# An mLSTM cell and a squared-ReLU FFN on one core: squares on ScalarE, wider rounding, and half-depth matmuls in quarters of the array

## The chip, the cores and the metric

The kernel runs on one core of one Trainium2 chip. The metric is the device time of one execution in microseconds (us), as the median of several executions. Times inside an execution come from one profiled run; they count from the start of its span.

## What is computed

The reference is an mLSTM cell over 768 time steps for 4 batches of 8 heads of 40 elements, and a feed-forward network (FFN) with a squared rectifier on its output, seen as 3072 tokens of 320 elements.

```python
for t in range(S):                       # q, k, v, o_gate: (4, 8, 768, 40)
    m_new = np.maximum(f_gate[:, :, t] + m, i_gate[:, :, t])
    f_stab = np.exp(f_gate[:, :, t] + m - m_new)
    i_stab = np.exp(i_gate[:, :, t] - m_new)
    m = m_new
    C = f_stab[..., None, None] * C + i_stab[..., None, None] * einsum('bhd,bhe->bhde', vt, kt)
    n = f_stab[:, :, None] * n + i_stab[:, :, None] * kt
    h_tilde = einsum('bhde,bhe->bhd', C, qt)
    denom = np.maximum(np.abs(einsum('bhd,bhd->bh', n, qt)[..., None]), 1.0)
    y[:, :, t] = sigmoid(o_gate[:, :, t]) * h_tilde / denom
...
x = y.transpose(0, 2, 1, 3).reshape(3072, 320)
h = np.maximum(x @ w_in, 0.0)            # w_in: (320, 2048)
out = h * h @ w_out                      # w_out: (2048, 320)
```

The two weights arrive as 64-bit words and are rounded to 32 bits inside the kernel.

## The kernel before

The time steps are cut into 24 chunks of 128 tokens, numbered `s`; six chunks make one batch, and `c` is the chunk's place in its batch. Inside a chunk the recurrence is written as attention. `scores(s)` multiplies keys and queries of eight heads, two heads at a time, because one head fills only 40 of the 128 rows of TensorE's array. `weigh` turns gate sums into weights on ScalarE (`mask` on GpSimd goes before it), `weighted` multiplies scores and weights on VectorE, `attend_turned` multiplies the result with the values and with the state `C`, `normalise_turned` divides by the denominator and applies the output gate.

From chunk 7 on, keys and queries come already paired through DRAM: `load_squares(s)` fetches 32x32 blocks with four DMAs, and `turn_kq(s)` transposes them in place on VectorE (L318). There are two such buffers, used by even and by odd chunks. `load_squares(s + 2)` is issued in stage `s` on SyncE's queue behind `store_rows(s)`, which waits for `normalise_turned(s)`.

The FFN works on groups `g` of two chunks. Its first product of groups 0 to 2 is written plainly: `ffn1_main` and `ffn1_rest` fill two PSUM banks, `relu_half` writes the rectified values into SBUF tiles `r_sb` on ScalarE (L671), and `square_half` squares them on VectorE into the tile of squares (L678). From group 3 on both products use Winograd's form of Strassen's scheme: seven products of halves instead of eight, with sums of blocks prepared on VectorE and GpSimd. `ffn1_open` and `ffn1_close` make the first product in two quarters `q`; each takes four PSUM banks X, Y, V and Z. The last 64 of the 320 rows of `w_in` go through 64-row matmuls in `ffn1_close` (L845), two at a time in the lower and upper half of the array's rows. `ffn2_fast` makes the second product in four steps with two banks in steps 0 and 1 and two more in steps 2 and 3.

`Rounding` brings the weights in as 26 pieces: ten of `w_in`, 512 columns wide, and sixteen of `w_out`, 320 columns wide. A piece costs a DMA on SyncE's queue (`fetch`), two ScalarE operations (L196, L198), three on VectorE (L207, L211, L212) and one on GpSimd (L216). The tuples `NEXT` and `LAST` say how many pieces must be done after each part of the early loop and of the main loop.

The order of the work is written out by hand: each engine executes its instructions in the order in which the program issues them. The main loop takes the chunks from `s = 6` on; a stage `s` has four quarters, `at` = 0 to 3. The FFN part of a stage alternates: from `s = 8`, even stages run `ffn2_fast` of one group, one step in each quarter, and odd stages from `s = 9` run `ffn1_open`, `ffn1_close`, `ffn1_open`, `ffn1_close` of another (`fast`). Around it stand the attention's parts: at 0 `scores(s)` and `weighted(s)`; at 1 `attend_turned(s)`, then, among others, `turn_kq(s + 1)` and `turn_squares(s - 1)` (L615), and the loads; at 2 `scale_q(s + 1)` (L486), `weigh(s + 1)`, `normalise_turned(s)` (L568 to L577), `store_rows(s)`, `load_squares(s + 2)`, `load_rows(s)`, `load_A(s + 2)`; at 3 the sums of blocks of `x` on GpSimd. Sums of blocks of the squares (`sums`, L734) are spread over the quarters on VectorE.

In the main loop PSUM's eight banks are three for attention (`ps_at`) and five for the FFN (`ps_h`, tile `h_ps`).

Of the kernel before, what the change touches and what calls it, by code (L numbers as in the profile page):

```python
# [29 lines left out]
def kernel(  # L30
# [127 lines left out]
            ))  # L158
    IN_DONE = (3, 5, 8, 10)
    assert len(pieces) == IN_DONE[-1]  # L160
    pieces += [(w_out[:, fb, :], [(slice(0, P), wout_w[fb * P : (fb + 1) * P])]) for fb in range(NF)]
    NRAW = 4

    class Rounding:
# [11 lines left out]
        def fetch(self):  # L176
            n = len(self.raws)
            if n == len(pieces):
                return
            dst, srcs = pieces[n]  # L180
            raw = conv.tile([P, 512, 2], I32, name="raw", bufs=NRAW)
            self.raws.append(raw)
            for rows, src in srcs:
                to = raw[rows, : dst.shape[1]]
                if len(src.shape) == 4:
                    to = to.rearrange("p (a f) w -> p a f w", a=src.shape[1])
                nc.sync.dma_start(to, src)

        def words(self):
            n = len(self.a)  # L190
            if n == len(pieces):
                return
            w = pieces[n][0].shape[1]
            raw = self.raws[n][:, :w]
            mag = conv.tile([P, 512], F32, name="mag", bufs=3)
            nc.scalar.activation(mag[:, :w], raw[:, :, 1].bitcast(F32), AF.Abs)  # L196
            low = conv.tile([P, 512], F32, name="low", bufs=3)
            nc.scalar.activation(low[:, :w], raw[:, :, 0].bitcast(U32), AF.Copy, bias=2.0, scale=2.0 ** -51)  # L198
            self.a.append((mag, low))

# [80 lines left out]

    SQ = 32
    KQ_SQ, X_SQ = 7, 6

    def pair_up(s):
        b, c = divmod(s, NB)
# [112 lines left out]
            )  # L399

    def bank(o=False):
        t = ps_o.tile([P, W], F32, name="tp", tag="o_ps") if o else ps_at.tile([P, W], F32, name="tp", tag="at")
        return t[:].rearrange("p (j t) -> p j t", j=PR)

    def transposes(s, o=(False, False)):
# [10 lines left out]
    def scores(s, o=(False, False)):  # L416
        d = st[s]

        sc = [bank(o[i]) for i in range(2)]
        for j in range(PR):  # L420
            for i in range(2):
                rows = slice(DP * i, DP * i + D)
                nc.tensor.matmul(  # L423
                    sc[i][:, j, :], lhsT=d["kT"][rows, j, :], rhs=d["qT"][rows, j, :], start=True, stop=True,
                )
        d["sc"] = sc

    def weighted(s):
        d = st[s]
# [235 lines left out]
    def relu_half():  # L665
        if "half" in st:
            hs, g4 = st.pop("half")
            rs = []
            for h in hs:
                rs.append(ffn.tile([P, 2, WG], F32, name="r_sb", bufs=4))  # L670
                nc.scalar.activation(rs[-1][:], h[:], AF.Relu)  # L671
            st.setdefault("relu", []).append((rs, g4))

    def square_half():
        if st.get("relu"):
            rs, g4 = st["relu"].pop(0)
            for i, r in enumerate(rs):
                nc.vector.tensor_tensor(g4[:, :, i, :], r[:], r[:], op=ALU.mult)  # L678

    def ffn2(g, j, part):  # L680
        if part == 0:
# [129 lines left out]
    def blocks(to, lhsT, rhs, q, start):  # L811
        for n in range(4):
            nc.tensor.matmul(  # L813
                to[:, n, :], lhsT=lhsT[:, 4 * q + n, :], rhs=rhs, start=(start and n == 0), stop=True,
                skip_group_check=True,
            )
# [13 lines left out]
        nc.vector.tensor_tensor(U4[:], V[:], U2[:], op=ALU.add)  # L830
        blocks(Z, F22, xs[:, 4, :], q, True)

    def ffn1_close(g, q):
        xT, xs = st["xT", g], st["xs"]
        (X, Y, V, Z), (U2, U4) = st["f1"], st["U"]
        g4 = st["g2", g][:, 8 * q : 8 * q + 8, :].rearrange("p (n two) t -> p n two t", two=2)
        t0, t1 = slice(0, P), slice(P, 2 * P)
        blocks(X, F12, xT[:, 0, 1, :], q, False)
        blocks(Y, F21, xs[:, 2, :], q, True)
        blocks(V, WS[3], xT[:, 1, 1, :], q, True)  # L840
        lo, hi = slice(0, KR), slice(KR, 2 * KR)
        for pair in (((X, lo, xT[lo, 0, 2, :]), (Y, hi, xT[hi, 1, 2, :])), ((V, lo, xT[lo, 1, 2, :]), (Z, hi, xs[hi, 1, :]))):
            for n in range(4):
                for to, rows, rhs in pair:
                    nc.tensor.matmul(  # L845
                        to[:, n, :], lhsT=w_in2[rows, 4 * q + n, :], rhs=rhs, start=False, stop=True, skip_group_check=True,
                    )
        tt = nc.vector.tensor_tensor
        nc.scalar.activation(g4[:, :, 0, t0], X[:], AF.Relu)
        tt(U2[:], U2[:], Y[:], op=ALU.add)  # L850
        tt(g4[:, :, 1, t1], U4[:], Y[:], op=ALU.add)
        tt(g4[:, :, 0, t1], U4[:], V[:], op=ALU.add)
        tt(g4[:, :, 1, t0], U2[:], Z[:], op=ALU.subtract)
        st["open"] = g4
# [97 lines left out]
    rounding.step()  # L952


    NEXT = (5, 8, 10, 11, 13, 15, 17, 19)
    for u in range(8):
        s = 2 + u // 2
        relu_half()
# [63 lines left out]
    for g in range(1, NG):  # L1022
        parts += [(2, g, i) for i in range(4)]
        if g + 2 < NG:
            parts += [(1, g + 2, i) for i in range(4)]
    LAST = (21, 23, 25, 25, 26)
    assert LAST[-1] == len(pieces)
    for n, (which, g, i) in enumerate(parts):
        s, at = 6 + n // 4, n % 4
        if n == 5:  # L1030
            brought.close()
            late = ctx.enter_context(tc.tile_pool(name="late", bufs=1, side="right"))
        if at == 0:
            do(score, s)
        if at == 1:
            do(attend_turned, s)
            do(decays, s + 1)
            do(mask, s + 1)
            if n > 4:
                do(turn_kq, s + 1)  # L1040
            do(decay_C, s + 1)
            if s > X_SQ:
                do(turn_squares, s - 1)
            do(store_num, s)
            do(load, s + 4)
            if 8 <= s < 20:
                load_o(s + 4)
            do(load_num, s)
            do(pair_up, s + 3)
# [15 lines left out]
                sums_of_win(2 * (n - 10) + more)  # L1065
        if at == 3 and s >= 8 and s % 2 == 0 and s // 2 - 1 < NG:
            sums_of_x(s // 2 - 1)
        fast = which == 1 and g > 2
        if at == 2 and not fast:
            if n > 4:  # L1070
                do(scale_q, s + 1)
        if at == 3:
            if s % 4 == 3:
                for r in range(s + 1, min(s + 5, NT)):
                    sigmoid(r)
        if fast:
            (ffn1_close if i % 2 else ffn1_open)(g, i // 2)
            if at == 2:
                do(scale_q, s + 1)
        elif which == 1:  # L1080
            ffn1_main(g, i)
            if i % 2 == 0:
                held = st["half"]
            else:

                both = held, st["half"]
                for more, half in enumerate(both):
                    ffn1_rest(g, i - 1 + more, half[0])
                for half in both:
                    st["half"] = half  # L1090
                    relu_half()
                    square_half()
        elif g == 0:
            ffn2(g, *divmod(i, 2))
        else:
            ffn2_fast(g, i)
# [46 lines left out]
```

## Time and profile before

| | |
|---|---|
| median of 8 runs | 517.49 us (515.95 to 519.15) |
| the profiled execution | 516.24 us |
| its span, first to last instruction | 514.5 us |
| VectorE busy | 368.2 us (72%) |
| ScalarE busy | 237.9 us (46%) |
| GpSimd busy | 113.2 us (22%) |
| L678, squares on VectorE | 24 operations, 12.9 + 5.7 us |
| L671, rectifier on ScalarE | 24 operations, 12.7 us |
| L423, scores | 384 records, 27.0 us |
| L845, 64-row matmuls of the FFN | 576 records, 36.9 + 19.0 us |

A matmul of 32-bit operands appears as two records, each with a weight load of its own (engine PEld). "Busy" is the time in which at least one instruction of the engine or group runs, so for matmuls that overlap it is less than the number times the mean. The ends of matmuls are modelled; their starts are not.

### The profile page before, as it was taken

Reading aid. Unit: us, or ns where it says so; the run is one execution under the profiler, and the core shown is the slowest. Engines: PE = TensorE matmul, PEld = TensorE weight load, DVE = VectorE, ACT = ScalarE, POOL = GpSimd, SP = SyncE. Lnnn points to the kernel's source line nnn. Section 1 sums busy time; section 2 is a strip of 40 time slices with the busy share of each in tenths; the row PEclk is TensorE's granted clock in tenths of the full one; section 3 lists DMA queues with packets and bytes.
Section 4 is the critical chain, followed back from the end, with each engine's and each line's share of the span. In section 5 each row is a group of like instructions: output and inputs, shape, how many; then the busy total and the mean of one; then the engine's idle time right before and its main releaser. Section 6 shows DMA issues by size and latency. Waiting matters only on the chain.

```text
span 514.5 us, 11946 instructions
## 1 busy us (share of the span) xinstructions
PE 504.4 (98%) x4648; PEld 462.4 (90%) x4649; DVE 368.2 (72%) x678; ACT 237.9 (46%) x496; POOL 113.2 (22%) x146
## 2 busy tenths in 40 slices
PE   8989999999999999999999999999999999999997
PEld 4877878886698999999999999999999999999997
DVE  8589988969979777677768777668669667544441
ACT  3766667552531642571641681550771642432400
POOL 3346633233213103112112111112112112020000
PEclk9997999999999999999999999999999999999999
DMA  9999599786585776785785685785755353100000
GB/s 187 230 213 195 161 161 198 184 190 127 131 160 104 166 150 119 174 157 105 168 154 111 169 155 115 174 164 95 176 118 102 108 117 82 49 9 27 1 27 27
DMA packets 238361, 67.64 MB, mean 131 GB/s; under 512 B 185729, under 2 KB 232833, under 8 KB 238305
## 3 DMA queue, kind: packets, MB, share of 16 engines
q1 hardware_dynamic: 238208, 66.68, 61.8%
q8 instruction: 37, 0.61, 0.5%
q10 hardware_dynamic: 96, 0.20, 0.1%
q14 instruction: 20, 0.16, 0.1%
HBM read 54.56 MB, written 17.86 MB: 141 GB/s over the span
## 4 chain that ended last, share of the span: by engine, by line
PE 82%; DVE 9%; issue 2%; ACT 2%; DMA 2%; SPq 1%; POOL 0%; DVEq 0%; ACTq 0%; POOLq 0%
PE h_ps L739 32%; PE h_ps L813 21%; PE h_ps L845 7%; PE h_ps L645 4%; PE tp L423 4%; PE numT L522 3%; PE h_ps L685 3%; PE numT L513 2%; DVE mag L211 2%; PE hp L461 1%; DMA A_bc<-a_rows 1%; PE h_ps L656 1%; DVE g_c L678 1%; DVE mag L207 1%; DVE mag L212 1%
## 5 line engine op out<-in xcount | busy, mean ns | idle before, releaser
L361 POOL TENSOR_SCALAR_AFFINE_SELECT A_bc<-A_bc 128x1024 f32<-128x1024 f32 x22 | 24.3, 1106 | 213.4 <-ACT kq L371 185.6
L371 ACT ACTIVATE kq<-A_bc 64x512 f32<-64x512 f32 x30 | 18.8, 628 | 74.9 <-DMA A_bc<-a_rows 74.7
L739 PE MATMUL h_ps<-T,S 128*128 128x160 f32 x352 | 51.4, 299 | 0.0
L739 PE MATMUL h_ps<-w_out,g 128*128 128x160 f32 x336 | 49.2, 303 | 0.0
L739 PEld LDWEIGHTS h_ps<-T,S 128*128 128x128 f32 x352 | 49.0, 190 | 0.0
L385 ACT ACTIVATE A_bc<-A_bc,b_T 128x128 f32<-128x128 f32 x144 | 44.0, 389 | 7.6 <-POOL A_bc L361 7.0
L739 PEld LDWEIGHTS h_ps<-w_out,g 128*128 128x128 f32 x336 | 46.1, 190 | 1.1
L645 PE MATMUL h_ps<-xT,w_in 128*128 128x256 f32 x192 | 45.9, 395 | 0.6 <-ACT xT L624 0.6
L645 PEld LDWEIGHTS h_ps<-xT,w_in 128*128 128x128 f32 x192 | 37.0, 198 | 6.6 <-ACT xT L624 0.9
L813 PE MATMUL h_ps<-xT,w_in 128*128 128x128 f32 x288 | 40.7, 284 | 0.3 <-ACT r_sb L826 0.3
L813 PE MATMUL h_ps<-xs,w_in 128*128 128x128 f32 x288 | 38.0, 275 | 0.0
L813 PEld LDWEIGHTS h_ps<-xT,w_in 128*128 128x128 f32 x288 | 34.9, 191 | 3.4 <-ACT r_sb L826 0.5
L755 DVE TENSOR_TENSOR y_sb<-y_sb,h_ps 128x160 f32<-128x160 f32 x44 | 14.0, 318 | 33.2 <-PE h_ps L739 33.1
L826 ACT COPY r_sb<-h_ps 128x512 f32<-128x512 f32 x18 | 10.5, 584 | 58.0 <-PE h_ps L813 58.0
L845 PE MATMUL h_ps<-xT,w_in 64*128 64x128 f32 x432 | 36.9, 280 | 0.0
L845 PEld LDWEIGHTS h_ps<-xT,w_in 64*128 64x128 f32 x432 | 33.4, 187 | 2.2
L813 PE MATMUL h_ps<-xs,WS 128*128 128x128 f32 x288 | 35.1, 275 | 0.0
L813 PEld LDWEIGHTS h_ps<-xs,w_in 128*128 128x128 f32 x288 | 35.1, 192 | 0.0
L813 PEld LDWEIGHTS h_ps<-xs,WS 128*128 128x128 f32 x288 | 33.6, 192 | 0.0
L739 PE MATMUL h_ps<-w_out,g_c 128*128 128x160 f32 x192 | 28.0, 302 | 0.0
L850 DVE TENSOR_TENSOR r_sb<-r_sb,h_ps 128x512 f32<-128x512 f32 x18 | 12.3, 686 | 21.7 <-PE h_ps L845 21.7
L423 PE MATMUL tp<-kqT 40*128 40x128 f32 x384 | 27.0, 280 | 0.0
(167 smaller groups left out, 1070.0 us busy)
## 6 DMA issues: line engine op xcount, KB each, us to landing
A_bc<-a_rows SPq DMA_DIRECT2D x22, 512.0 KB, 4.8
raw<-in_moe_w_out_dram SPq DMA_DIRECT2D x16, 320.0 KB, 3.5
num_rows<-tn SPq DMA_DIRECT2D x18, 256.0 KB, 4.3
kq<-num_rows SPq DMA_DIRECT2D x72, 64.0 KB, 2.2
kqT<-kq_rows SPq DMA_DIRECT2D x34, 128.0 KB, 3.4
raw<-in_moe_w_in_dram SPq DMA_DIRECT2D x8, 512.0 KB, 5.6
kq<-in_k_dram SPq DMA_DIRECT2D x24, 160.0 KB, 5.0
va<-in_v_dram SPq DMA_DIRECT2D x24, 160.0 KB, 5.1
```

What stands on the lines that cost most here:

```text
L361: nc.gpsimd.affine_select(A[:], A[:], compare_op=ALU.is_ge, fill=-1e30, base=0, pattern=[[0, H], [1, P]], channel_multiplier=-1,)
L371: nc.scalar.activation(e[rows], st[s]["A"][0][rows, PR * i : PR * (i + 1), :], AF.Exp)
L385: nc.scalar.activation(d["W"][:, i * n + h, :], A[i][:, h, :], AF.Exp, bias=b_T[:, b, c, i * n + h : i * n + h + 1],)
L423: nc.tensor.matmul(sc[i][:, j, :], lhsT=d["kT"][rows, j, :], rhs=d["qT"][rows, j, :], start=True, stop=True,)
L522: nc.tensor.matmul(numT[i][halves[g], e, :], lhsT=va_w[s % NKQ][:, h * D1 : h * D1 + DP], rhs=d["P"][h % 2][:, h // 2, :] if s < KQ_SQ els ...
L645: nc.tensor.matmul(hs[i][:, n, :], lhsT=w_in[:, a, fb * P : (fb + 1) * P], rhs=xT[:, :, a, :], start=(n == 0 and a == 0), stop=False,)
L685: nc.tensor.matmul(o_ps, lhsT=st["g2", g][:, fb, j * P : (j + 1) * P], rhs=w_out[:, fb, :], start=(fb == 0), stop=(fb == NF - 1),)
L739: nc.tensor.matmul(to, lhsT=lhsT[:, p], rhs=rhs[:, p, :], start=(start and p == 0), stop=(p == NPAIR - 1), skip_group_check=True,)
L755: add = lambda to, a, b: nc.vector.tensor_tensor(to, a, b, op=ALU.add)
L813: nc.tensor.matmul(to[:, n, :], lhsT=lhsT[:, 4 * q + n, :], rhs=rhs, start=(start and n == 0), stop=True, skip_group_check=True,)
L845: nc.tensor.matmul(to[:, n, :], lhsT=w_in2[rows, 4 * q + n, :], rhs=rhs, start=False, stop=True, skip_group_check=True,)
L850: tt(U2[:], U2[:], Y[:], op=ALU.add)
```

## The change

In five places:

1. `relu_half` writes the rectified values straight into the tile of squares, and `square_half` squares that tile in place with one ScalarE operation of 1024 columns. The VectorE multiplications and the use of `r_sb` here go.
2. `w_out`'s pieces are two blocks wide (640 columns), so there are 18 pieces in all; the rounding tiles grow to 640 columns, and `NEXT` and `LAST` are renumbered.
3. From chunk 7 on `scores` makes each matmul in two, of 64 keys each, so that four matmuls (two heads, two halves of the keys) address the four quarters of the array.
4. For even `s` from 8 on, the scores of the odd chunk `s + 1` move into stage `s`: `turn_kq(s + 1)` goes from quarter 1 to quarter 0, `scores(s + 1)` stands at the head of quarter 1, into two banks of `ps_h`, and `weighted(s + 1)` in quarter 3. The odd stage begins with the FFN.
5. The 64-row matmuls move into a function `ffn1_rows`, each in two halves of 64 columns, in the order of the four quarters. In the first half of an odd stage they go to the head of quarter 1, ahead of `attend_turned`, and they, not F21 and WS[3], then clear the banks Y and V.

```diff
-    pieces += [(w_out[:, fb, :], [(slice(0, P), wout_w[fb * P : (fb + 1) * P])]) for fb in range(NF)]
+    pieces += [
+        (
+            w_out[:, fb : fb + 2, :].rearrange("p a d -> p (a d)"),
+            [(slice(0, P), wout_w[fb * P : (fb + 2) * P].rearrange("(a p) c w -> p a c w", p=P))],
+        ) for fb in range(0, NF, 2)
+    ]
+    WIDE = 2 * DM
...
+    HALVES = slice(0, DP), slice(DP, 2 * DP)
...
     def bank(o=False):
-        t = ps_o.tile([P, W], F32, name="tp", tag="o_ps") if o else ps_at.tile([P, W], F32, name="tp", tag="at")
+        if o == "h":
+            t = ps_h.tile([P, W], F32, name="h_ps")
+        else:
+            t = ps_o.tile([P, W], F32, name="tp", tag="o_ps") if o else ps_at.tile([P, W], F32, name="tp", tag="at")
...
+        if s >= KQ_SQ:
+            for j in range(PR):
+                for keys in HALVES:
+                    for i in range(2):
+                        rows = slice(DP * i, DP * i + D)
+                        nc.tensor.matmul(
+                            sc[i][keys, j, :], lhsT=d["kT"][rows, j, keys], rhs=d["qT"][rows, j, :], start=(j == 0),
+                            stop=True, skip_group_check=True,
+                        )
+            return
...
-            rs = []
-            for h in hs:
-                rs.append(ffn.tile([P, 2, WG], F32, name="r_sb", bufs=4))
-                nc.scalar.activation(rs[-1][:], h[:], AF.Relu)
-            st.setdefault("relu", []).append((rs, g4))
+            for i, h in enumerate(hs):
+                nc.scalar.activation(g4[:, :, i, :], h[:], AF.Relu)
+            st.setdefault("relu", []).append(g4)
...
-            for i, r in enumerate(rs):
-                nc.vector.tensor_tensor(g4[:, :, i, :], r[:], r[:], op=ALU.mult)
+            nc.scalar.activation(g4, g4, AF.Square)
...
+    def ffn1_rows(g, q, first):
+        xT, xs = st["xT", g], st["xs"]
+        X, Y, V, Z = st["f1"]
+        lo, hi = HALVES
+        pairs = (
+            ((X, lo, xT[lo, 0, 2, :], False), (Y, hi, xT[hi, 1, 2, :], first)),
+            ((V, lo, xT[lo, 1, 2, :], first), (Z, hi, xs[hi, 1, :], False)),
+        )
+        for pair in pairs:
+            for n in range(4):
+                for cols in HALVES:
+                    for to, rows, rhs, start in pair:
+                        nc.tensor.matmul(
+                            to[cols, n, :], lhsT=w_in2[rows, 4 * q + n, cols], rhs=rhs,
+                            start=(start and n == 0), stop=True, skip_group_check=True,
+                        )
...
-        blocks(Y, F21, xs[:, 2, :], q, True)
-        blocks(V, WS[3], xT[:, 1, 1, :], q, True)
...
+        blocks(Y, F21, xs[:, 2, :], q, not begun)
+        blocks(V, WS[3], xT[:, 1, 1, :], q, not begun)
+        if not begun:
+            ffn1_rows(g, q, False)
...
-    NEXT = (5, 8, 10, 11, 13, 15, 17, 19)
+    NEXT = (5, 8, 10, 11, 12, 13, 14, 15)
...
-    LAST = (21, 23, 25, 25, 26)
+    LAST = (16, 17, 18, 18, 18)
...
+        even = s >= 8 and s % 2 == 0
+        fast = which == 1 and g > 2
         if at == 0:
-            do(score, s)
+            if s < 8 or even:
+                do(score, s)
+            if even:
+                do(turn_kq, s + 1)
         if at == 1:
+            if even:
+                do(lambda s: scores(s, ("h", "h")), s + 1)
+            if fast:
+                ffn1_rows(g, 0, True)
             do(attend_turned, s)
...
-            if n > 4:
+            if n > 4 and not even:
                 do(turn_kq, s + 1)
...
         if at == 3:
+            if even:
+                do(weighted, s + 1)
...
         if fast:
-            (ffn1_close if i % 2 else ffn1_open)(g, i // 2)
+            if i % 2:
+                ffn1_close(g, i // 2, i == 1)
+            else:
+                ffn1_open(g, i // 2)
```

## The prediction

> **What bounds the kernel now.** I read the page first, then the chain of waits, then VectorE's and SyncE's queues in one pair of stages.
>
> ```profile
> PE 504.4 (98%) x4648; PEld 462.4 (90%) x4649; DVE 368.2 (72%) x678; ACT 237.9 (46%) x496; POOL 113.2 (22%) x146
> ```
>
> TensorE is the bound, and the others have room on average. Modelled ends hide small gaps, so the chain from 218 to 260 us matters more (start, us, what; stages 12 and 13):
>
> ```profile
> 218.83 0.89 PE tp L423 x16
> 219.72 4.54 PE h_ps L739 x32
> 224.27 1.02 PE numT L522 x16
> ...
> 225.60 11.06 PE h_ps L739 x80
> 236.66 1.09 PE tp L423 x16
> 237.75 3.77 PE h_ps L813 x32
> 241.52 0.60 PE numT L513 x16
> 242.12 1.02 PE numT L522 x16
> ...
> 243.45 2.88 PE h_ps L813 x24
> 246.33 1.99 PE h_ps L845 x32
> ```
>
> The reader should see TensorE alone, without a gap, and the same durations in every pair. So each instruction saved on TensorE counts in full, and so does each wait put on it. Two waits are candidates. VectorE's timeline of the same stages:
>
> ```profile
> 226.37 1.25 DVE L318 STREAM_TRANSPOSE kqT<-kqT 128x1024 f32<-128x1024 f32 x1
> ...
> 234.53 0.32 DVE L755 TENSOR_TENSOR y_sb<-y_sb,h_ps 128x160 f32<-128x160 f32 x1 [0.72 <-PE h_ps L739]
> 234.77 0.17 DVE L568 TENSOR_SCALAR dm<-kq 128x8 f32<-128x8 f32 x1
> ...
> 237.28 1.22 DVE L734 TENSOR_TENSOR S<-S,g 128x1024 f32<-128x1024 f32 x1
> 238.42 0.32 DVE L755 TENSOR_TENSOR y_sb<-y_sb,h_ps 128x160 f32<-128x160 f32 x1
> 238.65 1.28 DVE L438 TENSOR_TENSOR A_bc<-tp,A_bc 128x512 f32<-128x512 f32 x2
> ```
>
> From 234.53 on VectorE works without a pause and is 2.7 us behind when it ends the first half of weighted(13). The keys for 13 are asked for late (issues of `load_squares` from 214 to 224 us):
>
> ```profile
> L311 SPq DMA_DIRECT2D kqT<-kq_rows x4: 491/694/884, 217.6 to 219.6; - x4
> DMA to landing us min/median/max: 2.9/3.9/4.3
> ```
>
> The last lands at about 219.6 + 3.9 = 223.5. Last, what a gap can cost (TensorE's timeline, then its granted clock second by second):
>
> ```profile
> 39.44 1.09 PE L454 MATMUL dC<-vw,kq 128*128 128x82 f32 x8 [1.25 <-DVE g_c L438]
> ```
>
> ```profile
> 42.00:43.00 1.00, 1.00 (x7) 0.50 1.16 267
> ```
>
> The clock reads 0.73 in 41:42, 0.50 until 48, 0.85 in 48:49: 3.4 us lost after one gap. Gaps of 1.22 us at 67.7 and 1.24 at 125.8 cost no clock.
>
> **What the skill says.** "TensorEngine Tiling (Array Packing)", Key Properties: changing the tiling mode drains the engine. The trace agrees: 32 records of L813 take 3.77 us, 56 take 6.45, so 112 ns each and 0.20 us more for each run of one shape. "TensorE: Matmul & The Clock Gate", Part 3: matmuls in distinct tiles run concurrently. L513 already runs in quarters: its 16 records start between 241.5 and 241.9 and the next line follows after 0.60 us, so four groups of four, about 0.11 us each after 0.16 for the change of shape. The same page, Part 1: the clock halves after an idle window of about 3.4 us; here a gap of 1.25 us, among matmuls of few columns, was enough, so the measurement decides. "ScalarE: Activation LUTs", What ACT_TABLE_LOAD costs: 186 ns + 0.833 ns a column, 1.04 us for 1024; L862 measures 1.045.
>
> **Part by part.**
>
> *Squares.* VectorE loses 24 operations of L678 (12.9 + 5.7 us). ScalarE gains 12 of 1.045, 12.5 us, at 46% load. *Wide pieces.* From the rows of 320 and 512 columns I extend to 640 (an estimate): VectorE 0.64 + 0.93 + 0.83 us against 2 x (0.40 + 0.58 + 0.49), so 0.54 less per pair of blocks, 4.3 us in all; ScalarE 3.4 us less, GpSimd about 1. DMAs: 8 of 640 KB for 16 of 320 KB, the same bytes. All this lies before 130 us, where VectorE is 8 to 10 tenths busy, but TensorE's chain is unbroken from 68 to 109 us and the gap at 39 us precedes the first square. What the path can win is two gaps: 1.22 us before L623 at 67.7 (VectorE was held by two squares of 2.36 us) and 1.7 before L513 at 125.8 (seven squares stand in the chain ahead of it). Bounds +1 (ScalarE's squares delay a rectifier) to -4; I take -2.5.
>
> *Quarters.* Four quarter matmuls do the work of two halves in the same 0.11 us, so the array gains nothing by itself: 48 groups a pair at 2 to 3 ns, 0.1 us. The gain is in runs of one shape. Before, a pair has scores(s+1), L813, L513, L813, L845, L813, L845 with the next scores, L739, L513, L739. After, scores(s+1) join L513 of the even stage, `ffn1_rows` joins L513 of the odd one, and the L739 and L813 around them join: four runs less, 0.8 us, and 0.04 because a quarter run costs 0.16. Sum 0.95 us a pair; eight pairs (8/9 to 22/23) 7.6, with the ninth FFN stage and chunk 7 about **-7.8 us**. I bound this between -9 and +9: if the sequencer can't feed a record every 27 ns over sixteen groups (L513 shows only four), a group at 0.15 us costs 0.04 x 424 groups = 17 us more.
>
> *turn_kq(s+1) moved to quarter 0.* In before it ran at 226.37, long after landing. Now scores(13) want it when step 0 ends, at 224.2. VectorE has ended weighted(12) by 221.7, waits for the landing at 223.5, and ends at 224.7: a wait of 0.5. `load_squares` was not moved. Stage 14: last issue 259.2, landing 3.0 later, transposed 263.4, wanted 262.1, so 1.3. Read alike for stages 8, 10, ... 22: 0.4, 1.9, 0.6, 1.4, 1.0, 0.5, 2.5, 2.4, sum 10.7. Queued behind the waiting transpose on VectorE: the sum A11 - A21 (1.22 us) and L755; step 1 needs that sum only in its second product, so it hides. Behind scores(s+1) on TensorE everything waits. The odd stage's `attend_turned` also comes 1.8 us later against its stage's end, because `ffn1_rows` goes first; from it follow store_num, load_num, normalise and then `load_squares`. SyncE's queue, busy with other issues until 244.7 where the numerator is ready at 243.7, hides 1.1. I add 0.2 for each of seven: **+12.1**; bounds 4 and 18.
>
> *weighted(s+1) moved to quarter 3.* It now stands ahead of L755 but behind the same normalise and sum, so it ends its first half at 239.1, 2.5 us after the stage's old start at 236.6. It holds two of five banks. Of the four that `ffn1_open` wants, X and Y can take banks freed earlier; V, two products of 0.9 us after the start, at 238.3, must have one of the two. Wait 0.8. The six later odd stages that I could read (11 to 21) give 0.1, 0.9, 0.9, 0.1, 0.9, 1.6; I add 0.5 for 23. Stage 9: three sums of weights lie ahead, L438's first half would end at 165.0, V is wanted at 161.2: 3.9, less the 1.0 that L513 waits there today. Sum 5.0 + 2.9 = **+7.9**; bounds 3, and 15 if the rotation of banks makes Y wait in V's place.
> `ffn1_rows` waits for U2 and U4 on VectorE (0.69 us each), which end about 0.3 us before they're wanted once V has waited: 0.
>
> *Clock.* Gaps of over 2 us in stages 9, 10, 20 and 22 are longer than the one that cost 3.4 us. I take two such losses, **+6.8**; bounds 0 and 17.
>
> Sum on the profiled execution: 516.2 - 2.5 - 7.8 + 12.1 + 7.9 + 6.8 = 532.7. It lies 1.25 below the median of the runs, so 534.0.
>
> **Rivals.**
> A. *The waits, but no loss of clock*, since one gap stands alone in before and dense matmuls surround the new ones: 527.2. Chance 0.30.
> B. *Not slower: the keys and weights arrive in time.* One mechanism: with 32 changes of shape fewer and VectorE freed of squares early, the stages settle so that the transposed keys of the odd chunk are there 5.5 us after the even chunk's scores start. It decides once the last block lands by 4.2 us after that start; today it lands at 4.6 to 6.7. Then only savings are left: 516.2 - 10.3 + 1.25 = 507.2. For it: the gain on TensorE is certain in kind. Against: the landing depends on a DMA that nothing moves. Chance 0.13.
> C. *Quarters do not run four at a time for long*, so the change doesn't do what it says: a further 17 us in place of the clock's 6.8: 544. For it: only four groups in a row are seen. Against: the starts in L513 show no slowing. Chance 0.09.
> D. *Waits of about the size of the savings*: 517.5, chance 0.06.
>
> **Numbers.** The forecast has 0.42. The median is 534.0; the range from 518 to 546 holds the forecast, A and nearly all of C, and leaves B and half of D out. The forecast's own range, from its bounds, is 526 to 544. What can be told from no change is 0.3%, 1.6 us. Faster: B and a quarter of D, 0.14; same: half of D, 0.04 with rounding; slower 0.82.
>
> **What would show it.** Right: scores at the head of quarter 1 wait for L318, and L318 for kqT's DMA, by 0.5 to 2.5 us in even stages; L813's V blocks wait for L438 in odd stages, most in stage 9; in odd stages the FFN's 64-row matmuls run straight into L513 without a change of shape; TensorE's clock falls in slices of the main loop. Wrong: an unbroken chain on TensorE with pairs of 37 us, or `ffn1_rows` taking over 2.2 us for its 64 records.

## The result, and the profile after

The changed kernel takes 529.02 us in the median of 11 runs (527.12 to 531.72), against 517.83 us of the kernel before in the 31 runs beside it: a ratio of 1.023, with an interval of 1.021 to 1.0249. It is slower by 11 us; 534.0 was forecast, in a range of 518 to 546. The profiled execution took 531.25 us, 2.2 above the median; its span is 529.5 us against 514.5 before, so the accounts below have 15.0 us of span to explain.

First the page of the changed kernel: the engines' busy time, and the clock that TensorE was granted in 40 slices.

```profile
PE 509.0 (96%) x5496; PEld 467.7 (88%) x5497; DVE 341.4 (64%) x630; ACT 248.5 (47%) x492; POOL 114.8 (22%) x138
...
PEclk9997999999997999979999999999989999999999
```

TensorE is still the bound, but its share fell from 98% to 96% of a longer span, and its clock has three new dents (the 13th, 18th and 30th digit) beside the old one. In each dent the clock that was granted fell to half of full speed for one or two stretches of 3.41 us; "half clock" below means this. There are 848 more records, the quarters, and VectorE and ScalarE changed about as they should: 27 us less and 11 more. The loss stands in TensorE's list of waits (total us, times, longest):

```profile
PE h_ps L436 <- issue: 7.4, 4, 2.8
PE h_ps L830 <- DVE A_bc L458: 4.3, 3, 3.7
```

L436 is the line of the scores (L423 before), here writing FFN banks (`h_ps`), so these are the moved scores of odd chunks. "Issue" means that the profile shows no releaser. The cause must be read from the timelines of stage 12. TensorE (start, us, what, and in brackets the idle time before it):

```profile
222.78 1.05 PE L436 MATMUL tp<-kqT 40*64 40x128 f32 x32
223.76 2.44 PE L756 MATMUL h_ps<-w_out,g 128*128 128x160 f32 x16
226.36 2.44 PE L756 MATMUL h_ps<-T,S 128*128 128x160 f32 x16 [0.16 <-ACT g L878]
231.62 2.10 PE L436 MATMUL h_ps<-kqT 40*64 40x128 f32 x32 [2.82 <-issue]
```

VectorE at the same time:

```profile
222.39 0.17 DVE L588 TENSOR_SCALAR dm<-kq 128x8 f32<-128x8 f32 x1 [4.18 <-DMA kq<-num_rows]
...
226.49 1.28 DVE L458 TENSOR_TENSOR A_bc<-tp,A_bc 128x512 f32<-128x512 f32 x2
230.27 1.25 DVE L325 STREAM_TRANSPOSE kqT<-kqT 128x1024 f32<-128x1024 f32 x1 [2.50 <-DMA kqT<-kq_rows]
```

And SyncE's queue, where a time is that of issuing:

```profile
212.78 0.38 SPq L571 DMA_DIRECT2D num_rows<-tn  x1
...
217.16 1.94 SPq L576 DMA_DIRECT2D kq<-num_rows  x4
...
224.21 0.38 SPq L623 DMA_DIRECT2D x_rows<-x_sb  x1
224.64 2.92 SPq L318 DMA_DIRECT2D kqT<-kq_rows  x4
```

Read backwards: the scores start at 231.62, 0.10 after the transpose L325 ends; that waited for squares asked for at 224.64, behind `store_rows` (L623); that waited for `normalise_turned` (L588 on), before which VectorE stood 4.18 us for stage 11's numerators. The scores were wanted at about 228.8, when step 0 of the FFN (L756) ended.

The other wait is nearly all in stage 9. TensorE there:

```profile
159.41 1.06 PE L830 MATMUL h_ps<-xs,WS 128*128 128x128 f32 x8
164.20 2.05 PE L830 MATMUL h_ps<-xs,WS 128*128 128x128 f32 x8 [3.74 <-DVE A_bc L458]
```

and VectorE:

```profile
161.10 1.22 DVE L814 TENSOR_TENSOR w_in<-w_in 128x1024 f32<-128x1024 f32 x1
162.24 1.22 DVE L816 TENSOR_TENSOR WS<-w_in,WS 128x1024 f32<-128x1024 f32 x1
163.38 1.28 DVE L458 TENSOR_TENSOR A_bc<-h_ps,A_bc 128x512 f32<-128x512 f32 x2
```

V needs a bank that holds scores of chunk 9, and `weighted(9)` (L458) frees it only behind the combining of `w_in`. Eight matmuls now take 2.05 us instead of 1.06: the clock has also halved (at 163.32).

From such timelines each pair of stages can be measured, from the start of the even stage's scores to that of the next even stage. All in us, each from one profiled execution, with the falls of the clock that this execution happened to have; the last five columns are the experiments 5, 8, 10, 11 and 12, told below:

| pair | before | after | squares on ScalarE's queue | and sums later | scores left, sums later | scores left, both mends | and transposes behind |
|---|---|---|---|---|---|---|---|
| 8, 9 | 39.61 | 44.91 | 44.66 | 42.75 | 38.76 | 40.20 | 39.49 |
| 10, 11 | 38.20 | 38.81 | 37.48 | 37.48 | 37.63 | 37.62 | 37.62 |
| 12, 13 | 37.92 | 44.30 | 38.85 | 38.68 | 37.73 | 37.98 | 37.33 |
| 14, 15 | 38.51 | 39.13 | 38.47 | 38.47 | 39.14 | 38.33 | 37.92 |
| 16, 17 | 38.21 | 37.68 | 37.49 | 37.48 | 37.62 | 37.63 | 37.62 |
| 18, 19 | 37.91 | 38.73 | 38.46 | 39.03 | 38.25 | 37.73 | 37.34 |
| 20, 21 | 39.13 | 42.15 | 39.00 | 39.00 | 38.77 | 38.34 | 38.04 |

After against before, these pairs and the last (38.30 to 39.04) are 17.0 us longer; the start of stage 8 came 1.8 sooner.

### The profile page after: what moved, and what is told of

It reads as the page before. It is cut to its first block, busy times and chain, and to the rows that moved or that the text cites. A ratio compares the mean times of both kernels' runs of the same rounds, so it can differ in the third digit from the quotient of the medians.

```text
span 529.5 us, 13526 instructions
## 1 busy us (share of the span) xinstructions
PE 509.0 (96%) x5496; PEld 467.7 (88%) x5497; DVE 341.4 (64%) x630; ACT 248.5 (47%) x492; POOL 114.8 (22%) x138
## 5 line engine op out<-in xcount | busy, mean ns | idle before, releaser
L368 POOL TENSOR_SCALAR_AFFINE_SELECT A_bc<-A_bc 128x1024 f32<-128x1024 f32 x22 | 26.4, 1200 | 220.2 <-ACT kq L378 184.0
L756 PE MATMUL h_ps<-T,S 128*128 128x160 f32 x352 | 51.5, 299 | 0.2 <-ACT g L878 0.2
L756 PE MATMUL h_ps<-w_out,g 128*128 128x160 f32 x336 | 50.8, 309 | 0.0
L756 PEld LDWEIGHTS h_ps<-T,S 128*128 128x128 f32 x352 | 49.0, 190 | 0.4 <-ACT g L878 0.4
L756 PEld LDWEIGHTS h_ps<-w_out,g 128*128 128x128 f32 x336 | 47.6, 195 | 1.5 <-issue 1.2
L830 PE MATMUL h_ps<-xs,WS 128*128 128x128 f32 x288 | 38.2, 283 | 5.1 <-DVE A_bc L458 4.3
L559 DVE STREAM_TRANSPOSE tn<-numT 128x256 f32<-128x256 f32 x36 | 15.9, 450 | 41.3 <-PE numT L542 41.3
L830 PEld LDWEIGHTS h_ps<-xs,WS 128*128 128x128 f32 x288 | 35.0, 195 | 7.1 <-issue 4.0
L830 PE MATMUL h_ps<-xT,w_in 128*128 128x128 f32 x288 | 38.9, 278 | 0.0
L830 PE MATMUL h_ps<-xs,w_in 128*128 128x128 f32 x288 | 38.9, 279 | 0.0
L862 PE MATMUL h_ps<-xT,w_in 64*64 64x128 f32 x864 | 36.5, 280 | 0.0
L830 PEld LDWEIGHTS h_ps<-xT,w_in 128*128 128x128 f32 x288 | 35.2, 192 | 0.9 <-issue 0.7
L830 PEld LDWEIGHTS h_ps<-xs,w_in 128*128 128x128 f32 x288 | 35.9, 196 | 0.0
L862 PEld LDWEIGHTS h_ps<-xT,w_in 64*64 64x64 f32 x864 | 32.2, 137 | 2.3 <-issue 0.2
L325 DVE STREAM_TRANSPOSE kqT<-kqT 128x1024 f32<-128x1024 f32 x17 | 21.1, 1240 | 16.0 <-DMA kqT<-kq_rows 15.8
L756 PE MATMUL h_ps<-w_out,g_c 128*128 128x160 f32 x192 | 28.0, 302 | 0.0
```

Of the source, the lines that this page charges most:

```text
L325: nc.vector.transpose(t, t)
L368: nc.gpsimd.affine_select(A[:], A[:], compare_op=ALU.is_ge, fill=-1e30, base=0, pattern=[[0, H], [1, P]], channel_multiplier=-1,)
L559: nc.vector.transpose(to[:, 2 * i : 2 * i + 2], numT[i][:, :2, :].rearrange("p c t -> p (c t)"))
L756: nc.tensor.matmul(to, lhsT=lhsT[:, p], rhs=rhs[:, p, :], start=(start and p == 0), stop=(p == NPAIR - 1), skip_group_check=True,)
L830: nc.tensor.matmul(to[:, n, :], lhsT=lhsT[:, 4 * q + n, :], rhs=rhs, start=(start and n == 0), stop=True, skip_group_check=True,)
L862: nc.tensor.matmul(to[cols, n, :], lhsT=w_in2[rows, 4 * q + n, cols], rhs=rhs, start=(start and n == 0), stop=True, skip_group_check=True,)
```

## The experiments

A ratio is to the kernel before in the same batch, whose medians were 517.73 in the first four, 517.55 in the next four, 517.46 in the next three, 516.50 in the last.

**1. The early edits alone.** The kernel before with the squares, the wide pieces and their tuples, and nothing else.

```diff
-                nc.vector.tensor_tensor(g4[:, :, i, :], r[:], r[:], op=ALU.mult)
+            nc.scalar.activation(g4, g4, AF.Square)
...
-    LAST = (21, 23, 25, 25, 26)
+    LAST = (16, 17, 18, 18, 18)
```

> The kernel before with the squares on ScalarE and the wide pieces of w_out alone; all matmuls as before. Theory W (waits: the two early edits help a little, the loss comes from moved work that waits for a DMA and for VectorE): the second chunk-8 stage begins 1.8 us sooner, as in the changed kernel, and nothing later changes, so 516.0 against 517.8, ratio 0.9965. Rival E (the loss begins early, ScalarE being loaded with squares): 518 or more.

Measured: 515.26 us, ratio 0.9947 (0.9927 to 0.9967). The early edits are worth 2.5 us.

**2. Quarters in place.** The kernel before with scores and 64-row matmuls cut into quarters, each where its halves stood: `ffn1_rows(g, q, False)` is called within `ffn1_close` for every quarter.

> The kernel before with the scores from chunk 7 on and the FFN's 64-row matmuls in quarters of the array, each where it stood; nothing moved. Theory W: a group of four quarters takes 109 ns where a pair of halves takes 112, and 424 groups give 1.0 us, with little more or less at the changes of shape: 516.3 to 517.8, ratio 0.997 to 1.000. Rival Q (quarters cost TensorE time by themselves, in records to issue or in changes of shape): over 519, ratio above 1.003.

Measured: 517.95 us, ratio 1.0006 (0.999 to 1.0022). Four quarters cost what two halves cost, to within 0.2% of the kernel's time.

**3. The odd scores not moved.** The changed kernel without the move of `turn_kq`, `scores` and `weighted` of odd chunks.

```diff
-            if s < 8 or even:
-                do(score, s)
-            if even:
-                do(turn_kq, s + 1)
+            do(score, s)
...
-            if even:
-                do(lambda s: scores(s, ("h", "h")), s + 1)
```

> The changed kernel with the odd chunk's scores, transpose and weighting back in the odd stage; squares, wide pieces, quarters and the moved 64-row matmuls stay. Theory W: no wait for the keys' DMA in even stages and none of VectorE in stage 9 beyond the 1.0 us of before, TensorE's clock stays up in the main loop, the moved 64-row matmuls still save two changes of shape in eight stages: 517.8 - 1.8 - 3 = 513, ratio 0.990. Rival M (moving the 64-row matmuls ahead of the attention is itself a loss, since it delays the chain through DRAM): 518 or more, with waits in odd stages or at the next even stage.

Measured: 515.41 us, ratio 0.9956 (0.9926 to 0.9986), and no fall of the clock in the main loop. So the move of the odd scores costs 529.02 - 515.41 = 13.6 us, more than the whole loss. But 513 was expected: the result equals that of the early edits alone, so the quarters and the moved 64-row matmuls gain nothing net. Its trace has a wait of 2.05 us of the 64-row matmuls in stage 9 and 0.4 to 1.8 us in the middle of other odd stages.

**4. The squares sooner, on SyncE's queue.** `load_squares(s + 2)` ahead of `load_num(s)` in quarter 1.

```diff
+            do(load_squares, s + 2)
             do(load_num, s)
...
             do(store_rows, s)
-            do(load_squares, s + 2)
```

> The changed kernel with the loads of the keys' squares issued in quarter 1, ahead of the numerator's reload, in place of quarter 2 behind the store of x. Theory W: the waits of TensorE between step 0 and the moved scores, 8.9 us in the changed kernel's profile, go, and with them the two falls of the clock that follow them (5.1 us); the wait and the fall in stage 9 (5.9 us) stay: 529.0 - 14 = 515, ratio 0.995. Rival C (the clock falls for another reason, or the transposed keys wait for VectorE's other work): 523 or more.

Measured: 537.61 us, ratio 1.0392 (1.0344 to 1.0439): 8.6 us slower than the changed kernel, where 14 faster was expected. SyncE's queue of this run shows it:

```profile
236.50 3.45 SPq L318 DMA_DIRECT2D kqT<-kq_rows  x4
239.99 3.65 SPq L576 DMA_DIRECT2D kq<-num_rows  x4
```

Four issues occupy the queue for 3.45 us, and now the numerators' reloads wait behind them. VectorE's and TensorE's waits (total us, times, longest):

```profile
DVE dm L588 <- DMA kq<-num_rows: 43.5, 14, 6.2
```

```profile
PE h_ps L830 <- DVE A_bc L458: 12.9, 6, 4.1
PE h_ps L436 <- issue: 7.5, 4, 2.7
```

VectorE waits 43.5 us for the numerators instead of 10.2, and what stands behind on VectorE, `weighted(s + 1)` and the next transposes among it, is late. The wait was only passed on. The experiment did not test the place of the squares alone, because it also put off another transfer.

**5. The squares sooner, on ScalarE's queue.** Again in quarter 1, but from another queue.

```diff
-                nc.sync.dma_start(
+                (nc.scalar if s > KQ_SQ else nc.sync).dma_start(
...
             do(attend_turned, s)
+            do(load_squares, s + 2)
...
             do(store_rows, s)
-            do(load_squares, s + 2)
```

> The changed kernel with the loads of the keys' squares issued from ScalarE's queue in quarter 1, ahead of the decays, so that they come a stage sooner and SyncE's queue issues four DMAs fewer in each stage. Theory W2 (the moved scores wait for the keys' DMA; loading them sooner on SyncE's own queue failed only because their 3 us of issue pushed back the reload of the numerator): no wait for the keys' DMA, no fall of the clock after stage 9, 529.0 - 14 = 515. Rival V (the even stages wait because VectorE is late with everything, whatever the keys' landing): VectorE's waits for the numerator or its own backlog take the DMA's place and the time stays at 523 or more. ScalarE's issue time, 3 us a stage, may cost a little in either.

Measured: 518.68 us, ratio 1.0028 (1.0008 to 1.0048): 10.3 us of the 13.6 come back, 3.7 less than was expected. Stage 12 of this run, VectorE:

```profile
222.93 1.28 DVE L458 TENSOR_TENSOR A_bc<-tp,A_bc 128x512 f32<-128x512 f32 x2
224.13 1.23 DVE L325 STREAM_TRANSPOSE kqT<-kqT 128x1024 f32<-128x1024 f32 x1
225.28 1.18 DVE L751 TENSOR_TENSOR g<-g 128x1024 f32<-128x1024 f32 x1
```

No wait in brackets: the keys have landed, and the pair 12, 13 takes 38.85 us instead of 44.30. "PE h_ps L436 <- issue" is gone from the list of waits, the moved scores start 5.53 us after those of their even stage in seven stages of eight (5.58 in stage 8) where it was 5.6 to 8.8, and the clock falls once in the main loop, in stage 9. The issue isn't free on ScalarE:

```profile
227.49 2.82 ACTq L318 DMA_DIRECT2D kqT<-kq_rows  x2
230.34 1.28 ACT L378 ACT_TABLE_LOAD   x1 [2.10 <-issue]
```

ScalarE stood 2.10 us for two issues. And now waits for `weighted` show in odd stages where the changed kernel has none or less: L830's first run takes 1.10 us too long in stage 13, 0.71 in 19 and 0.81 in 21.

**6. The combining of `w_in` later.** The changed kernel with the second half of these sums (L814, L816) issued at the start of quarter 1 of stage 9, not in quarter 3 of stage 8.

```diff
-        if n in (10, 11):
+        if n == 10:
             for more in range(2):
-                sums_of_win(2 * (n - 10) + more)
+                sums_of_win(more)
...
+            if n == 13:
+                sums_of_win(2)
+                sums_of_win(3)
```

> The changed kernel with the last two sums of w_in's blocks (two VectorE operations of 1.2 us) moved from quarter 3 of stage 8 to the head of quarter 1 of stage 9, so that weighted(9) comes 2.4 us sooner. Theory W: the wait of 3.8 us in stage 9 for PSUM banks that weighted(9) frees shrinks to about 1.5 us, and with it goes the fall of the clock at 163 us: 5 us in all, 524. Rival (that stage is late for another reason, the DMA of x or GpSimd's sums): 528 or more.

Measured: 528.36 us, ratio 1.022 (1.0187 to 1.0254), not the 524 of the theory. Stage 9 itself did as the theory says: L830's excess falls from 5.49 us, its half clock within, to 1.10, and the pair 8, 9 from 44.91 to 39.94. But in its profile the pair 10, 11 rose to 41.09 and 18, 19 to 43.51, each with a new fall of the clock. The cause of stage 9's wait is shown; its gain didn't stay while the keys were late.

**7. The 64-row matmuls not moved.** The changed kernel with the first quarter's `ffn1_rows` back in `ffn1_close`.

```diff
-            if fast:
-                ffn1_rows(g, 0, True)
             do(attend_turned, s)
...
-                ffn1_close(g, i // 2, i == 1)
+                ffn1_close(g, i // 2, False)
```

> The changed kernel with the FFN's 64-row matmuls back behind the other blocks of the first half (in quarters, but not ahead of the attention); the scores stay moved. Theory W: the keys land late anyway, the shift by the moved matmuls is some 0.2 us a stage, so the waits of the even stages stay within 3 us of 8.9, and two more changes of shape a pair cost 3: 526 to 532. Rival M (the moved matmuls delay the attention by 2 us, through DRAM the normalisation, and through it the keys' load; that is the cause of the waits): the waits fall by more than half and with them the clock's falls, 520 or less.

Measured: 529.94 us, ratio 1.0262 (1.0217 to 1.0307). So the moved 64-row matmuls don't make the kernel late. From the scores' starts, beyond the 5.53 us of run 5, the even stages wait 8.8 us in all here and 9.3 in the changed kernel, though not in the same stages: stage 12 waits 1.4 here, 3.3 there (counted so, a stop of 0.3 us within step 0 is included).

**8. The edits of runs 5 and 6 together.**

> Both repairs together: keys loaded from ScalarE's queue, and the two sums of w_in's blocks later. Theory W2: what is left is the savings, 0.6 us a pair on TensorE and 2 us early, with 0.4 us of bank waits in some odd stages: 517.8 - 2 - 4.8 = 511, ratio 0.987. Rival V: 518 or more.

Measured: 516.77 us, ratio 0.997 (0.9954 to 0.9986). Both mends together take 12.3 us off, but 511 is missed by 5.8. This run's waits of TensorE:

```profile
PE h_ps L830 <- DVE A_bc L458: 4.6, 5, 1.8
```

With the keys in time, `weighted` of the odd chunk is what comes late: in five stages, the most in stage 9 (1.8 us, then 3.41 us at half clock).

**9. The wait filled with idle matmuls.** The changed kernel with nine of them, on zeros, ahead of the moved scores of stages 12 and 20.

```diff
+            if s in (12, 20):
+                idle(9)
             if even:
                 do(lambda s: scores(s, ("h", "h")), s + 1)
```

> The changed kernel with nine idle matmuls (one column of zeros broadcast, into a bank of their own) put into TensorE's queue ahead of the moved scores of stages 12 and 20, where TensorE waited 2.9 and 2.25 us and the clock halved for 6.83 and 3.41 us. They compute nothing that is read. Theory (the gap in TensorE's work is what halves the clock): both falls after those two stages are gone while the waits stay, since the keys land no sooner; 5.1 us come off, 529.0 -> 524, ratio to before about 1.013. Rival (the clock falls for the narrow matmuls around the gap, or on a timetable, not for the gap): the falls stay and the idle matmuls cost up to 1 us: 529 to 531.

Measured: 533.34 us, ratio 1.0299 (1.0271 to 1.0328): 4.3 us slower than the changed kernel, so the 524 failed. The clock stayed whole after both filled waits, as the theory says, but it fell in stages 16, 18 and 22, where it had not in the changed kernel's profile; and in stage 12 step 0 itself stood 1.59 us for ScalarE (L878), ahead of the idle matmuls, where it stood 0.16 in the changed kernel, so that the moved scores came 9.06 us after the start of step 0, not 7.86. Why step 0 stood longer isn't shown. The run is no clean test of the clock; its windows are used below.

**10. Scores left, sums later.** The edits of runs 3 and 6 together.

> The changed kernel with the odd stages' scores left in their own stage, and the second half of the combining of w_in two quarters later. Theory: what kept the run with the scores left in their place (515.41) from its 513 or better was stage 9's 2.05 us wait of the 64-row matmuls for VectorE, which those sums delay; it goes, and the 0.4 to 1.8 us bank waits of the odd stages stay: 513, ratio 0.992. Rival (the cost moves with the sums into stage 9's second half): 515.5, ratio 0.996.

Measured: 513.01 us, ratio 0.9915 (0.9889 to 0.9942), 2.4 us below run 3. Stage 9's wait is gone, and the waits in the middle of the odd stages (0.40 to 1.21 us) are what is left.

**11. Scores left, both mends.** The edits of runs 3, 5 and 6.

> The same, and the loads of the squares on ScalarE's queue a quarter sooner. With the scores left in their place nothing waits for the squares, so this adds about 0.3 us of issuing on ScalarE for each of four transfers and stage. Theory (the squares' place matters only through the moved scores): 513 to 515, not below the run without it. Rival (SyncE's queue being freer brings the numerators and x back sooner, and the bank waits shrink): 511 or less, ratio 0.987.

Measured: 512.21 us, ratio 0.9902 (0.9879 to 0.9925). It can't be told from run 10, so a SyncE queue with four issues fewer in each stage, which run 5 has too, gains nothing by itself that can be told. Against run 8, which differs only in the move of the scores, it is 4.6 us faster, and the intervals do not touch: even with both mends, the move doesn't pay here, since the waits for V's bank that it brings stay.

**12. The transposes behind.** Run 11 with two transposes of squares issued after the FFN's first `ffn1_close` in odd stages, not ahead of it.

```diff
-            if n > 4:
+            if n > 4 and not fast:
                 do(turn_kq, s + 1)
...
-            if s > X_SQ:
+            if s > X_SQ and not fast:
                 do(turn_squares, s - 1)
...
                 ffn1_close(g, i // 2, i == 1)
+                if i == 1:
+                    do(turn_kq, s + 1)
+                    do(turn_squares, s - 1)
```

> The run with the scores left in their place, the sums later and the squares on ScalarE's queue (512.21), and in the odd stages of the fast FFN the two transposes of squares (1.25 and 0.54 us on VectorE) put behind the four operations that close the first quarter of the FFN's hidden rows, where they stood ahead. Theory: the 0.4 us that TensorE waits for a bank in the middle of each odd stage's long run of 128-row matmuls comes from those transposes, which hold VectorE when the first quarter's last products are done; five waits go, 2.0 us: 510.2, ratio 0.986. Rival (ScalarE's rectifier of X, not VectorE, frees the bank that is waited for): 512, ratio 0.990.

Measured: 509.40 us, ratio 0.9871 (0.9833 to 0.9908): the lowest median of all, but the interval overlaps that of run 11, so the times alone don't show the gain. The traces show its cause. Stage 13 of run 11 on VectorE, then on TensorE:

```profile
244.34 1.25 DVE L325 STREAM_TRANSPOSE kqT<-kqT 128x1024 f32<-128x1024 f32 x1
245.51 0.54 DVE L635 STREAM_TRANSPOSE xT<-xT 128x384 f32<-128x384 f32 x1
246.08 0.69 DVE L879 TENSOR_TENSOR r_sb<-r_sb,h_ps 128x512 f32<-128x512 f32 x1
246.68 0.68 DVE L880 TENSOR_TENSOR g_c<-r_sb,h_ps 128x512 f32<-128x512 f32 x1
```

```profile
246.29 1.06 PE L830 MATMUL h_ps<-xT,w_in 128*128 128x128 f32 x8
247.51 1.69 PE L830 MATMUL h_ps<-xs,WS 128*128 128x128 f32 x13 [0.17 <-DVE g_c L880]
```

The same of run 12:

```profile
245.16 0.69 DVE L879 TENSOR_TENSOR r_sb<-r_sb,h_ps 128x512 f32<-128x512 f32 x1 [1.28 <-PE h_ps L830]
245.77 0.68 DVE L880 TENSOR_TENSOR g_c<-r_sb,h_ps 128x512 f32<-128x512 f32 x1
```

```profile
245.85 1.06 PE L830 MATMUL h_ps<-xT,w_in 128*128 128x128 f32 x8
246.75 1.95 PE L830 MATMUL h_ps<-xs,WS 128*128 128x128 f32 x16
```

L880 is the last reader of the bank Y, which the later of the two groups of matmuls writes. In run 11 L880 ends at 247.36 and the group starts at 247.51, 1.22 us after the one ahead of it; in run 12 L880 ends at 246.45, and the starts are 0.90 us apart (245.85 to 246.75). The bracket shows only 0.17 of that wait, since the ends of matmuls are modelled; starts show it all. ScalarE's rectifier of X (L878) ends at 248.45 in run 11, after the group has begun, so it isn't what frees the bank. The long run of L830 in stages 9, 13, 15, 19 and 21 takes 9.53 us in run 11 and 9.13 in run 12.

## Why the prediction was right, and where its sum was not

The sign, its cause and the place of the waits were right. On the profiled execution 532.7 was forecast and 531.25 came. The forecast of the median, 534.0, is 5.0 us too high, because it took the profiled execution to lie 1.25 us under the median, as before; it lies 2.2 over it. Its mean clock was 0.977, that of the other ten executions 0.980 to 0.990. By the prediction's steps:

- **Squares and wide pieces, -2.5.** Right: 515.26 against 517.73 alone; 1.8 in the changed kernel's own profile.
- **Fewer changes of shape, -7.8, at 0.95 us a pair.** Right in size, but a part is taken back. The pair 10, 11 of run 5, which has no long wait, takes 37.48 us against 38.20, so 0.72 less; with the odd scores left in their place it is 0.58 less (37.62). By the prediction's count two of the four runs saved, 0.40 us, belong to the move of the scores, but only 0.14 remains. TensorE's starts show where the rest goes: in every odd stage V's blocks start 0.15 us after the first half of `weighted` has ended (204.88 and 204.73 in stage 11 of run 5). So V starts 1.04 us after Y, and Z 0.97 after V, where each step is 0.89 with the scores left in place. That is 0.23 us a stage, and 0.72 + 0.23 is the 0.95 forecast. Why Z is late too isn't shown. That quarters by themselves change little agrees with run 2.
- **`turn_kq(s + 1)` waits for its DMA, 12.1.** The mechanism was right and is shown by run 5; the term was too large, 8.9 us from TensorE's starts: 0.0, 1.2, 2.9, 0.5, 0.1, 0.6, 2.3, 1.3 for stages 8 to 22, against 0.4, 1.9, 0.6, 1.4, 1.0, 0.5, 2.5, 2.4. The sum is nearer than its terms. Stage 12, said to cost 0.6, cost most, because VectorE stood 4.18 us for stage 11's numerators, which carries through the whole chain to the squares.
- **`weighted(s + 1)` holds V's bank, 7.9.** Right for stage 9: 3.9 was worked out and 3.74 measured. The 1.0 that was taken off, TensorE's wait in stage 9 of the kernel before, is indeed gone. There the chain of work ran through `weighted`:

```profile
164.68 0.61 DVE A_bc L438
165.34 0.66 PE numT L513 x14
```

L513 needed 1.59 us from its first start to the next line's, where it needs 0.60 in stage 11. In the changed kernel the same line (L533) needs 0.54 in stage 9.

For the stages after it the term was too large. 5.0 was said; beyond the 0.15 counted above, which fits the 0.1 read for stages 11 and 17, only stages 15 and 19 wait, 0.3 each. With the keys in time, stages 13, 19 and 21 of run 5 waited 0.7 to 1.1 us more each, as 0.9 to 1.6 was read for them. The prediction added two waits as if they were independent; the likely reading is that a TensorE that stands for keys gives VectorE and the numerators' transfers the time to catch up. No run tests this alone. ScalarE's issuing is not the reason in stage 13 of run 5: `weigh(13)` had ended at 236.55, 5.6 us before `weighted(13)` began.
- **Not in the sum: the bank Y.** Five odd stages of the changed kernel lose 0.4 us in the middle of L830's run, 2.0 in all, because VectorE transposes squares before it frees the bank (run 12). `ffn1_rows` was expected to wait for nothing, and it doesn't, but moving it ahead lets the next products want their banks that much sooner: with it back in its place (run 7) no stage shows the loss.
- **Clock, two falls, +6.8.** Three falls in the main loop, of 6.83, 6.83 and 3.41 us at half speed: half of 17.1 is 8.5 us at most, since a wait fills a part of that time. The number was fair for this execution; the other executions, at their higher mean clocks, lost less. Its reason, the length of a gap, is not what the traces show (below).

The measured terms, -1.8 - 8 x 0.95 + 8.9 + (3.74 - 1.0 + 0.6 + 8 x 0.23) + 2.0 + 8.5, make 15.2 us against the 15.0 of the span. The prediction's make 16.5. So near a sum is luck in part: its two waits are 5.9 us too high together, and the other terms, with the bank Y left out, 4.6 too low.

Rival A's 527.2 is nearer to the median than the forecast, but its reason, no loss of clock, is refuted by the profile. Rival B failed twice over: the keys came late, and with the keys in time (run 5) the kernel takes 518.68, not 507.2, because `weighted` is late next and the bank Y is freed late. Rival C is refuted: `ffn1_rows` starts its 64 records and gives way to the next line after 1.80 us, sixteen groups of four at 0.11 us each, as "TensorE: Matmul & The Clock Gate", Part 3, lets one expect of matmuls in distinct tiles. Rival D is out.

Left open: why the changed kernel's later even stages wait by such different amounts from one version to the next (stage 18: 0.6 us in the changed kernel, 2.2 in run 6), and whether the move would pay with both mends if only stage 9's scores stayed in their place. Neither was measured.

## What to carry to other kernels

Before a consumer is moved forward, follow its operand back through every transfer to the queue that issues it: here a net 0.14 us of TensorE's time a pair, 1.1 in all, was bought with 8.9 us of waits, because the request for the keys stayed behind a store. To mend such a wait, mind the queue and not only the order, since a request put ahead of others on the same queue passes the wait on to them (run 4). And waits on two engines should not simply be added: here waits of 0.7 to 1.1 us for VectorE in three stages were 0.3 or less while TensorE stood for the keys, and came up once the keys were in time.

## What the runs showed of the hardware

The prediction took a gap's length as what halves the clock. The falls in a profile lie a multiple of 3.413 us apart: in the changed kernel they are at 163.32, 231.59 and 392.01, so 20 and 47 times 3.413. So the time can be cut into windows on that grid. Windows of the changed kernel just before a possible fall (length, then each engine's busy time; the clock within the window; DMA):

```profile
159.91:163.32 3.41, 0.56 (x5) 0.37 (x4) 3.41 (x4) 0.29 (x1) 0.00 (x0) 1.00 0.65 106
187.22:190.63 3.41, 2.35 (x18) 2.11 (x16) 1.28 (x2) 3.19 (x5) 0.00 (x0) 1.00 0.61 127
228.18:231.59 3.41, 0.62 (x5) 0.38 (x4) 1.32 (x2) 3.18 (x4) 0.00 (x0) 1.00 0.75 96
388.60:392.01 3.41, 1.62 (x50) 1.48 (x50) 2.59 (x3) 3.18 (x4) 0.00 (x0) 1.00 0.67 171
429.56:432.97 3.41, 2.15 (x51) 1.94 (x53) 2.58 (x3) 2.33 (x3) 0.00 (x0) 1.00 0.76 180
```

The first number after the comma is TensorE. The windows with 0.56, 0.62 and 1.62 us of work were followed by half speed, those with 2.35 and 2.15 were not. Two windows of run 9 fit: the filled one of stage 12, which was not followed by half speed, and one in stage 16 that was:

```profile
229.48:232.89 3.41, 2.78 (x41) 1.58 (x41) 2.58 (x3) 1.92 (x2) 0.00 (x0) 1.00 0.54 134
307.99:311.40 3.41, 1.79 (x40) 1.58 (x42) 2.35 (x3) 3.40 (x5) 0.00 (x0) 1.00 0.70 138
```

Over all 14 profiles, from 60 us to the last window that has a whole one behind it, the windows at full clock count so, by TensorE's busy time:

| busy in the window | windows | followed by half clock |
|---|---|---|
| under 1.5 us | 7 | 7 |
| 1.5 to 1.95 us | 16 | 9 |
| 1.95 to 2.25 us | 13 | 1 |
| over 2.25 us | 1799 | 0 |

Before 60 us this does not hold. Each of the 14 profiles has one fall there, and in 12 of them the window ahead of it had 2.3 to 2.9 us of TensorE's work. In the kernel before it is the window that holds the prediction's gap of 1.25 us:

```profile
38.07:41.47 3.40, 2.15 (x21) 2.06 (x19) 3.06 (x6) 0.28 (x1) 2.31 (x2) 1.00 0.67 167
```

Half speed followed here, and did not follow the window at 429.56 with the same 2.15 us. The matmuls here have 82 and 41 columns (L447 to L461); whether that is the reason isn't shown. So busy time as the profile counts it sorts the windows of the main loop, and is not the whole rule.

"TensorE: Matmul & The Clock Gate", Part 1, says that the window is 3413 ns and runs freely; the traces agree. It speaks of an idle window; here windows with about half their time at work were enough in 9 of 16 cases, and the measurement decides. So in the main loop a gap of 1.5 to 2 us, which leaves 1.4 to 1.9 us of work in a window, costs clock or not by where it falls. With the mean clocks of 11 executions of one kernel between 0.977 and 0.990, a forecast of such a loss can only be a chance.
